# Key and query products of the state joined to two Gram products, and the second joins to the other two, in a fused DeltaNet and maxout kernel

## The chip, the cores and the metric

The kernel runs on one core of one Trainium2 chip. The metric is the device time of one execution in microseconds. Before the change, three runs took 506.8 us in the median (504.97 to 507.69). The profile is of one further look at an execution on that core, whose span from the first to the last instruction is 505.2 us.

The engines are called by short names: PE is TensorE (PEld its weight loads), DVE is VectorE, ACT is ScalarE, POOL is GpSimd, SP is SyncE, which issues most of the DMAs. PSUM is the memory that PE writes its products to, SBUF the one that all engines work in.

## The reference

Two blocks, one behind the other. First a DeltaNet recurrence over 768 positions, for 4 batches of 8 heads with 48 dimensions each:

```python
k_n = k / (norm(k) + 1e-06)
for t in range(S):
    y[t]  = q[t] @ state
    v_old = k_n[t] @ state
    state = state + beta[t] * outer(k_n[t], v[t] - v_old)
```

Then `y`, with its heads side by side, is a matrix `x` of 3072 tokens by 384, and a maxout layer follows:

```python
h = maximum(maximum(x @ w1, x @ w2), x @ w3)   # 384 -> 768
out = h @ w_out                                # 768 -> 384
```

All is float32.

## The kernel before

**Chunks.** The sequence is cut into 12 chunks of 64 positions (`C = 64`). A chunk `c` holds two units, `n = 2c + g`: a unit is one chunk of half of the batches, so there are 24 units. Within a chunk the recurrence is turned into matrix products: a Gram matrix of the keys with themselves and with the queries, a triangular system, and products with the state that the chunk before left.

**Periods.** The maxout layer works on 512 tokens at a time, which is two chunks of all batches. So there are six periods, `m = 0` to `5` (`GROUPS = 6`). `ffn(m)` is a generator for the layer of period `m`; at each `yield` the main loop (L1505 to L1525) emits what a table tells it for that step. While the layer of period `m` runs, the recurrence of period `m + 1` (its chunks `2m + 2` and `2m + 3`) is done, and the units of period `m + 2` are prepared. So every engine's order of work is written out by hand: the order in which the program emits the instructions is the order on each engine's queue.

**The layer's steps.** In the periods 1 to 4, steps 0 to 11 are one hidden product each (`hidden`, L1217): three matmuls of 128x128 weights with 512 columns into `p_h` (the profile has two records for each float32 matmul, so six). Even steps are followed by a relu on ACT (L1234), odd ones by a maximum on DVE (L1238), which free the PSUM buffer; `p_h` has two buffers. Behind them come the products with `w_out` into `p_o`. In period 1, steps 2 and 5 have twelve records of `p_m` (L905) in addition, put between the hidden product and the table's names.

**The names of the tables.** Each is a letter and a number. Those that the change moves, and those around them:

- `k0` (`old_k`, L750): the keys of the period's first chunk times the state, 64 records of 48x64 tiles into `p_k`, and a subtraction on DVE (L755) that makes the right side. Nothing is done for it on a DMA queue.
- `q0` (`old_q`, L759): the same with the queries, 64 records into `p_q`, and a copy on ACT (L763).
- `g0` to `g3` (`gram`, L404): the Gram products of four units to come; the even ones 32 records of 128 columns, the odd ones 64 of 64 columns, into `p_g`. Then the mask on DVE (L399), a copy to `at` on ACT (L432), and four DMAs on SP (L445) that write `at` to memory.
- `t0` to `t3` (`turn_blocks`, L384): four transposes on DVE that make the `kqt` of the unit whose Gram product follows.
- `z0 z1` (`join_z`, L706): 64 records of 32x32 tiles each into `p_z`, and two copies on ACT.
- `j0 j1` (`join_u`, L719): the second joins, 64 records of 32x32 tiles each into `p_j`, and two ACT instructions each (L728) that write the negated product into `ut`.
- `d0 d1` (`turn_t1`): transposes on DVE that `j0 j1` read.
- `u0` (`new`, L765): the solved values, 64 records into `p_u`; it reads `ut` (behind `j0`) and the right side (behind `k0`).
- `s0`, `y0`, `k1`, `q1`, `u1` and so on: the state's step, the outputs, and the same for the second chunk.
- `L3`, `N0` to `N2`: loads of units to come (`load_blocks`, a memset and DMAs on POOL, partly on SP). `V0 V1`: loads of values.

At step 6 of a period `blocks` (L487) reads the Grams of `at` back in another layout into `x_bl`, on SP; at step 8 `solve` (L507) begins on them, a long row of small DVE instructions (L561, L565) which go on through the rest of the period.

**PSUM.** All of the recurrence's products take one of three buffers in turn (`ps_two`, tag `two`, L92). A product has to wait until what was in its buffer three products before has been read.

**The table.** `LINKS` (L1380) serves the periods 1 and 2. `FOURTH_LINKS` (L1385) serves period 3 and takes its steps 0 to 13 from `LINKS`. Period 0 has `EARLY_LINKS`, period 4 has `LAST_LINKS`; in period 5 nothing is left to do for the recurrence.

## Time and profile before

| | |
|---|---|
| three runs | 506.8 us median, 504.97 to 507.69 |
| profiled execution | 505.2 us span; its time outside the span is not shown |
| PE busy | 484.0 us, 8064 matmuls and 8064 weight loads |
| DVE busy | 361.1 us |
| ACT busy | 169.4 us |
| POOL busy | 187.1 us |
| TensorE's granted clock | 0.968 in the mean |
| the three changed periods start | at 158.35, 242.56 and 315.32 us |

The page tells for each engine how long it was busy. Further views answer for a stretch of time: the timeline lists an engine's instructions merged by line (start, length, engine, line, operation, output and inputs, tile shape, count, and in brackets the idle time before it with what ended it); the DMA view tells of each queue's packets, with their number, their megabytes and the time that they took as a share of 16 DMA engines over the stretch. Matmuls overlap in PE's pipeline, so the length of a group contains the tail of its last one, and the distance from a group's start to the next one's start is the better measure. The word "issue" stands for idle time in which an engine waited for nothing that the profile shows.

### The profile page before, as it was taken

Reading aid. Unit: us, or ns where it says so; the run is one execution under the profiler, and the core shown is the slowest. Engines: PE = TensorE matmul, PEld = TensorE weight load, DVE = VectorE, ACT = ScalarE, POOL = GpSimd, SP = SyncE. Lnnn points to the kernel's source line nnn. Section 1 sums busy time; section 2 is a strip of 40 time slices with the busy share of each in tenths; the row PEclk is TensorE's granted clock in tenths of the full one; section 3 lists DMA queues with packets and bytes.
Section 4 is the critical chain, followed back from the end, with each engine's and each line's share of the span. In section 5 each row is a group of like instructions: output and inputs, shape, how many; then the busy total and the mean of one; then the engine's idle time right before and its main releaser. Section 6 shows DMA issues by size and latency. Waiting matters only on the chain.

```text
span 505.2 us, 18676 instructions
## 1 busy us (share of the span) xinstructions
PE 484.0 (96%) x8064; PEld 338.0 (67%) x8064; DVE 361.1 (71%) x835; ACT 169.4 (34%) x320; POOL 187.1 (37%) x311
## 2 busy tenths in 40 slices
PE   7678989999999999999999999999999999999996
PEld 6467767855566555565565565555797457998895
DVE  5888799787996441799652999565998874468753
ACT  5585664885422142210152200242201032212210
POOL 7434472793391935770395880501000020000000
PEclk9855899999999999999999999999999999999999
DMA  8937869864045934544584652744224230340002
GB/s 114 205 50 214 195 142 160 198 181 137 3 120 134 191 72 77 146 119 117 112 156 104 158 137 74 149 72 96 64 54 90 47 86 15 85 94 1 0 18 47
DMA packets 109121, 53.50 MB, mean 106 GB/s; under 512 B 92208, under 2 KB 102864, under 8 KB 109040
## 3 DMA queue, kind: packets, MB, share of 16 engines
q1 hardware_dynamic: 97280, 31.78, 31.0%
q0 software_dynamic: 9216, 19.85, 16.5%
q8 instruction: 63, 1.03, 0.9%
q10 hardware_dynamic: 2544, 0.69, 0.8%
q14 instruction: 18, 0.15, 0.1%
HBM read 39.17 MB, written 13.11 MB: 103 GB/s over the span
## 4 chain that ended last, share of the span: by engine, by line
PE 76%; DVE 11%; ACT 4%; DMA 3%; SPq 3%; issue 2%; POOL 0%; DVEq 0%; ACTq 0%; POOLq 0%
PE p_h L1224 28%; PE p_o L985 13%; PE p_o L1262 12%; PE p_c L1163 5%; DVE tmp L561 3%; PE p_g L415 2%; PE p_m L905 2%; PE p_u L771 2%; PE p_k L743 2%; DVE y_p L565 2%; DMA kmore<-in_k_dram 2%; PE p_y L813 2%; PE p_s L794 2%; PE p_q L743 1%; PE p_j L726 1%
## 5 line engine op out<-in xcount | busy, mean ns | idle before, releaser
L1224 PE MATMUL p_h<-xt,w_sb 128*128 128x512 f32 (+1 forms) x450 | 186.8, 558 | 0.6 <-ACT xt L839 0.6
L1224 PEld LDWEIGHTS p_h<-xt,w_sb 128*128 128x128 f32 x450 | 82.4, 193 | 69.2 <-issue 61.6
L1238 DVE TENSOR_TENSOR h<-h,p_h 128x512 f32<-128x512 f32 (+1 forms) x42 | 25.5, 607 | 46.8 <-PE p_h L1224 46.3
L565 DVE TENSOR_TENSOR y_bl<-y_bl,tmp 128x31 f32<-128x31 f32 (+20 forms) x139 | 50.4, 363 | 4.8
L561 DVE TENSOR_TENSOR tmp<-x_bl,y_bl 128x31 f32<-128x31 f32 (+20 forms) x139 | 48.8, 351 | 3.9
L1262 PE MATMUL p_o<-wo_sb,h 128*128 128x384 f32 x144 | 48.9, 490 | 0.0
L373 POOL DMA_DIRECT2D turned<-in_q_dram x72 | 39.3, 554 | 4.6 <-POOL turned L368 3.1
L1262 PEld LDWEIGHTS p_o<-wo_sb,h 128*128 128x128 f32 x144 | 26.7, 190 | 17.2
L1234 ACT ACTIVATE h<-p_h 128x512 f32<-128x512 f32 x24 | 14.3, 597 | 69.2 <-PE p_h L1224 69.2
L263 POOL TENSOR_TENSOR w_sb<-mant,up 128x384 int32<-128x384 int32 x18 | 19.0, 1054 | 39.5 <-DVE mant L259 37.8
L415 PEld LDWEIGHTS p_g<-kqt 48*64 48x64 f32 x1216 | 24.5, 142 | 9.2 <-issue 6.3
L415 PE MATMUL p_g<-kqt 48*64 48x64 f32 (+1 forms) x1216 | 27.7, 241 | 0.9 <-ACT kqt L344 0.8
L1268 ACT COPY o_sb<-p_o 128x384 f32<-128x384 f32 x12 | 5.8, 479 | 62.6 <-PE p_o L1262 56.5
L801 DVE TENSOR_TENSOR st<-st,p_s 48x768 f32<-48x768 f32 (+1 forms) x18 | 17.1, 949 | 12.7 <-PE p_s L794 12.4
L399 DVE TENSOR_TENSOR pt<-p_g,mask 128x512 f32<-128x512 f32 x20 | 13.8, 690 | 17.0 <-PE p_g L415 16.9
L598 POOL DMA_DIRECT2D ut<-y_d x4 | 2.6, 653 | 60.6 <-DMA y_d<-y_bl 60.6
L148 POOL DMA_DIRECT2D v_t<-in_v_dram x14 | 11.6, 832 | 35.3 <-PE p_u L771 35.3
L368 POOL MEMSET turned<- 128x96 f32 x18 | 3.3, 191 | 49.4 <-DVE kqt L389 49.4
L771 PEld LDWEIGHTS p_u<-v_t,ut 64*64 64x64 f32 x768 | 13.5, 141 | 8.4 <-issue 7.3
L432 ACT COPY at<-p_g 128x512 f32<-128x512 f32 x22 | 12.8, 585 | 17.4 <-DVE pt L399 15.4
L373 POOL DMA_DIRECT2D turned<-in_k_dram x32 | 17.5, 556 | 1.2 <-POOL turned L368 1.2
L1163 PE MATMUL p_c<-xt,w_sb 128*128 128x256 f32 x72 | 17.7, 379 | 0.0
(239 smaller groups left out, 907.3 us busy)
## 6 DMA issues: line engine op xcount, KB each, us to landing
w_bits<-in_moe_w_dram SPq DMA_DIRECT2D x9, 384.0 KB, 6.2
w_bits<-in_moe_w_dram POOLq DMA_DIRECT2D x9, 384.0 KB, 5.7
turned<-in_q_dram POOLq DMA_DIRECT2D x72, 48.0 KB, 2.8
out_dram<-o_sb SPq DMA_DIRECT2D x36, 96.0 KB, 2.3
y_x<-y SPq DMA_DIRECT2D x32, 96.0 KB, 3.0
qall<-y_x SPq DMA_DIRECT2D x32, 96.0 KB, 2.8
v_t<-in_v_dram POOLq DMA_DIRECT2D x14, 192.0 KB, 5.0
at_d<-at SPq DMA_DIRECT2D x72, 32.0 KB, 3.0
```

The source lines that it names most:

```text
L263: nc.gpsimd.tensor_tensor(out=dst.bitcast(I32), in0=mant_v.bitcast(I32), in1=up_v, op=ALU.add)
L373: (queue, nc.gpsimd)[i].dma_start(out=t[p0 : p0 + 32, bb, at : at + NP * 2 * D].rearrange("p (j x) -> p j x", j=NP), in_=(k, q)[i][2 * bb ...
L415: nc.tensor.matmul(p_g[rows(bb ^ (g * i)), par, c0 : c0 + C * (1 + whole)], kq[:, 0], kq if whole else kq[:, i],)
L561: nc.vector.tensor_tensor(out=t_v, in0=row.to_broadcast(t_v.shape), in1=column.to_broadcast(t_v.shape), op=ALU.mult,)
L565: nc.vector.tensor_tensor(out=rest, in0=rest, in1=t_v, op=ALU.subtract)
L771: nc.tensor.matmul(p_v[rows(bb ^ g), g, i], ut[c % NU][rows(bb), g, h], rhs[rows(bb), g, h],)
L801: nc.vector.tensor_tensor(out=s_v[r], in0=s_v[r], in1=p_s[r, :, 0 : H * D], op=ALU.add)
L985: nc.tensor.matmul(to[:, g], a[j][:, 128 * g : 128 * (g + 1)], b[j], start=(start and g == j == 0), stop=(stop and g == 1 and j == len(a) ...
L1163: nc.tensor.matmul(to, w[stays], moves, start=(n == 0), stop=(n == len(terms) - 1))
L1224: nc.tensor.matmul(p_h, w_sb[i][:, t, f * 128 : (f + 1) * 128], xt[:, t, lo : lo + w], start=(t == 0), stop=(t == KT - 1),)
L1238: nc.vector.tensor_tensor(out=h, in0=h, in1=p_h, op=ALU.max)
L1262: nc.tensor.matmul(p_o, stays, moves, start=(n == 0), stop=(n == len(terms) - 1))
```

## The change

Four names move in `LINKS`. `k0 q0` leave step 0 and stand in front of `g0 g1` in step 2; `j0 j1` leave step 4 and stand in front of `g2 g3` in step 5. Their order among themselves and towards the other products stays. Between two hidden products the recurrence puts a run of small tiled products on PE; a period had ten such runs and now has eight. Since `FOURTH_LINKS` takes over the steps 0 to 13, the change holds for the periods 1, 2 and 3.

```diff
     LINKS = {
-        0: "k0 q0 t0 L3", 1: "t1", 2: "g0 g1 t2", 3: "z0 z1 d0 d1", 4: "j0 j1 t3 V0",
-        5: "g2 g3 p1", 6: "u0 N0", 7: "V1 N1", 8: "s0 y0 N2", 9: "x0", 10: "k1 q1",
+        0: "t0 L3", 1: "t1", 2: "k0 q0 g0 g1 t2", 3: "z0 z1 d0 d1", 4: "t3 V0",
+        5: "j0 j1 g2 g3 p1", 6: "u0 N0", 7: "V1 N1", 8: "s0 y0 N2", 9: "x0", 10: "k1 q1",
         11: "u1 w0", 13: "y1 x1 s1", 14: "X0 w1", 16: "P0", 17: "X1 K0 K1 K2 K3",
     }
```

No function changes.

## The prediction

> **What bounds the kernel now.** I read the page first, then the chain of waits, then TensorE's timeline through one period, then the packets that bring TensorE its instructions.

> ```profile
> span 505.2 us, 18676 instructions
> PE 484.0 (96%) x8064; PEld 338.0 (67%) x8064; DVE 361.1 (71%) x835; ACT 169.4 (34%) x320; POOL 187.1 (37%) x311
> ...
> q8 instruction: 63, 1.03, 0.9%
> ...
> PE 76%; DVE 11%; ACT 4%; DMA 3%; SPq 3%; issue 2%; POOL 0%; DVEq 0%; ACTq 0%; POOLq 0%
> ```

> PE is busy for 96% of the span, and from 131 us on the chain that ended last lies on PE almost alone, so whatever PE gains or loses in the three changed periods reaches the end. The third line is the one that I weigh most. 63 packets of 16 KB (1.03 MB / 63) stand against 8064 weight loads and 8064 matmuls: 16128 / 63 = 256 instructions a packet. TensorE is fed in blocks of 256.

> The second of the three changed periods, on PE:

> ```profile
> 245.23 1.15 PE L743 MATMUL p_k<-st,kqt 48*64 48x48 f32 x64
> 246.20 1.11 PE L743 MATMUL p_q<-st,kqt 48*64 48x48 f32 x64
> 247.24 5.42 PE L1224 MATMUL p_h<-xt,w_sb 128*128 128x512 f32 x12
> 252.59 2.09 PE L415 MATMUL p_g<-kqt 48*64 48x128 f32 x96
> 254.61 2.84 PE L1224 MATMUL p_h<-xt,w_sb 128*128 128x512 f32 x6
> 257.38 1.35 PE L713 MATMUL p_z<-ut,at 32*32 32x32 f32 x128
> 258.66 2.84 PE L1224 MATMUL p_h<-xt,w_sb 128*128 128x512 f32 x6
> 261.43 1.63 PE L726 MATMUL p_j<-z,t 32*32 32x32 f32 x128
> 263.00 2.84 PE L1224 MATMUL p_h<-xt,w_sb 128*128 128x512 f32 x6
> 265.77 2.09 PE L415 MATMUL p_g<-kqt 48*64 48x128 f32 x96
> ```

> Each row starts where the one before ends: PE waits for no engine here. Two things are to be seen. A run of p_h between tiled runs takes 2.77 us for six records, while twelve in one piece take 5.35, not 5.54. And the tiled rows hold many short instructions: p_j has 128 matmuls and as many loads, 256 instructions or one whole block, in 1.4 to 1.6 us, where p_h needs 2.77 us for twelve. The p_j row is also uneven: 1.39, 1.56 and 1.42 us from its start to the next row in the three periods, against 1.28 for p_z of the same shape.

> One stall shows what can lie behind that:

> ```profile
> 63.73 0.91 PE L771 MATMUL p_u<-v_t,ut 64*64 64x48 f32 x47
> 65.65 0.49 PE L771 MATMUL p_u<-v_t,ut 64*64 64x48 f32 x17 [1.01 <-issue]
> ```

> PE stops for 1 us in the middle of p_u and waits for nothing that the profile names. Counted in order of time (loads, matmuls and PE's own waits), the instruction behind the gap is number 2753 = 11 x 256 - 63. The largest gap inside the p_j of 261.43 (0.19 us, at 261.87) is at 9409 = 37 x 256 - 63, and the one inside the p_j of 334.19 (at 334.95) at 11969 = 47 x 256 - 63. Three gaps at one place of the block are no accident: PE came to a block that was not there yet. The packets before them, in narrow windows of the DMA view (62.8 to 64.5 us, then 259.1 to 260.5):

> ```profile
> q8 instruction: 1, 0.02, 5.5%
> ...
> q8 instruction: 1, 0.02, 4.9%
> ```

> 5.5% of 16 engines over 1.7 us is a packet of 1.5 us, 4.9% over 1.4 us one of 1.1. They landed at 64.38 and 260.32; PE went on at 65.65 and 261.87, 1.27 and 1.55 us later.

> **The change part by part.** It adds and removes no instruction; k0 q0 and j0 j1 go behind later steps of p_h in three periods (m = 1, 2 and 3; the others have tables of their own).

> What leaves PE. Starts of p_h are 0.429 us apart, 0.523 before a tiled run and 0.533 after one (+0.094, +0.104). The last p_q is followed by p_h after 0.148 us, but p_k by p_q after 0.038 (+0.110); the first four p_g take 0.140, later ones 0.089 (+0.051). Joining k, q and g saves all four, 0.36 us. Joining j and g saves the first two, 0.20 us: where a p_j of 32x32 tiles is followed directly by a 48x64 product (61.16 us) its exit costs 0.121 and the entry 0.035 more, as towards p_h. So 0.56 a period, 1.67 us in three; 2.15 at most if p_j to p_g were free as well.

> What comes. Runs of 448 instructions (k q g g: 128+128+192; j j g g: 256+192) in 3.9 and 3.4 us, where none before was over 256 without a p_h behind it in these periods. Price of a block, from the three gaps: block entered to next packet's start 1.51 (261.87 to 263.38), 1.29 and 1.19, mean 1.33; a packet 1.27 (mean of the six around the gaps, 1.11 to 1.50); landing to use 1.41 (the two above). Together 4.0 us. The packets often start before PE reaches the block, in slow p_h by some 40 instructions, which inside a tiled run is worth 0.25 us. So a block that PE runs through in less than 3.75 us makes it wait for the rest. Before, neighbouring blocks of the stretch are entered 3.99 to 4.95 us apart at the tightest (177.19 to 181.18, 257.69 to 261.87 to 266.27, 330.82 to 334.95): just enough.

> I moved the records into the new order and marked every 256th. First period: blocks begin at the end of q and near the end of j (120th of 128), and p_h steps stand inside both: 5.0 and 5.3 us, no wait. Second: one begins at the 23rd matmul of j, the next at the 21st of g: 1.14 + 0.15 + 0.58 = 1.87 us, a wait of 1.9. Third: 50th of k to 50th of g, 0.21 + 0.93 + 0.99 + 0.26 = 2.4, a wait of 1.35; 61st of j to 60th of g, 2.35, a wait of 1.4. Sum 4.65 us. A fourth pair (11th of k to 11th of g in the second period, 2.0 us) is asked for while p_h still runs, so I take 0 for it; without that lead it costs 1.7. With the quickest terms seen (0.8 + 0.93 + 1.27 = 3.0 us) the three come to 1.6; with the slowest (4.3 us) and the fourth, to 7.7. The waits fall in g; p_h, the relu and max behind it and the z or u products wait with PE, nothing overtakes.

> [...]

> Costed at nothing, with their cover:

> ```profile
> 246.50 0.95 DVE L755 TENSOR_TENSOR v_t<-v_t,p_k 128x768 f32<-128x768 f32 x1 [2.33 <-PE p_k L743]
> 262.42 2.40 ACT L728 ACTIVATE ut<-p_j 32x512 f32<-32x512 f32 x4 [0.29 <-PE p_j L726]
> 280.47 0.26 ACT L270 ACTIVATE root_bl<-x_bl 128x32 f32<-128x32 f32 x1 [1.85 <-DMA x_bl<-at_d]
> 285.12 0.68 DVE L1238 TENSOR_TENSOR h<-h,p_h 128x512 f32<-128x512 f32 x1
> ```

> The pool of three PSUM buffers is taken in the same order as before, but closer. g1 takes p_k's: free 1.27 + 0.95 = 2.2 us after k starts, wanted after 0.97 + 0.93 + 0.99 = 2.9. g3 takes p_j0's: free after two of ACT's four 0.6 us copies, 2.2, wanted after 2.5. If ACT were one copy late, 0.3 us a period. g2's copy to `at` starts behind those four, 3.4 us after j starts, and its mask on DVE ends then too, so the DMA of the Grams and x_bl move by 0 to 0.2 us; x_bl's root is needed at 280.86, and the max that frees p_h ends at 285.80 for a matmul at 286.16, so 0.36 us covers that. The moved products issue no DMA, so the order on SP's and POOL's queues stays. t0's transposes lose k0's 0.95 us in front of them; POOL's memset behind them and its loads start earlier, beside the loads of ut, which end by 256.0 (last issue 251.75, slowest landing 4.2) for a z at 257.38: 1.4 us of cover. u needs j0 and k0 only after another p_h.

> Sum: -1.67 + 4.65 = +3.0 on the profiled span of 505.2, so 508.2. The three runs have a median of 506.8 (504.97 to 507.69), 1.6 above that span, so 509.8.

> **The rivals.** (1) The blocks come in time, because more than one is held ahead: 506.8 - 1.7 = 505.1, not slower. It decides if a block takes under 1.9 us from entry to use of the next. For it: 384 instructions in one piece at 124.7 to 127.7 us (p_k, p_y, p_q) show no gap. Against it: only one block's edge falls in that piece, and the three gaps. If the uneven p_j (0.11 + 0.28 + 0.14 us over p_z) became even and p_j to p_g were free, 2.15 + 0.53 = 2.7, so 504.1. [...] (2) A PSUM buffer or x_bl is late in place of blocks: three times 0.3 to 0.6 us against 1.7, so 506.0 to 506.9. Nothing in the rows is late yet. (3) All block edges find slow packets, four waits: -1.7 + 7.7 = +6.0, so 512.8; it is the far end of my own case.

> **How the numbers follow.** Blocks late: 0.72, from 506.7 (-1.67 + 1.6) to 512.8, likeliest 509.8. Rival 1: 0.22. Rival 2: 0.06. 0.5% is 2.5 us, about what a measurement of this kernel can tell from no change. Late blocks give 0.66 slower and 0.06 within; rival 1 0.12 within and 0.10 faster; rival 2 0.06 within. The range 505.0 to 512.8 leaves out half of rival 1 and a little at the top; the likeliest case alone is 507 to 512.8.

> **What would show it.** Right: p_h runs of eighteen and twelve records in one piece, p_k and p_q before p_g without a gap; then gaps of 1 to 2 us marked issue inside p_g of the second and third period, an instruction packet ending 1.3 to 1.6 us before each ends. Wrong: p_g still 2.0 us after p_q and p_j (rival 1), or p_g released by ACT or DVE (rival 2).

## The result

The changed kernel takes 514.83 us in the median of six runs (511.67 to 518.16), the kernel before 507.22 us (504.97 to 508.74, six runs): a ratio of 1.0159, 95% interval 1.0121 to 1.0197. It is slower by 1.6% or 7.6 us, where +3.0 us (509.8 us) were predicted, and it lies above the range's end of 512.8 us. The profiled execution took 511.67 us, the least of the six; its span is 510.0 us.

From the page of the changed kernel, the lines that answer to the first fence of before:

```profile
span 510.0 us, 18668 instructions
PE 484.1 (95%) x8064; PEld 338.5 (66%) x8064; DVE 364.0 (71%) x835; ACT 168.9 (33%) x320; POOL 187.1 (37%) x311
...
q8 instruction: 63, 1.03, 0.9%
...
PE 81%; DVE 6%; DMA 5%; issue 2%; SPq 2%; ACT 2%; POOL 0%; DVEq 0%; ACTq 0%; POOLq 0%
```

PE is busy for as long as before (484.1 us against 484.0); the span is longer. So PE works no slower in this execution, it waits more. The timeline of PE in the second period shows where (start, length, engine, line, operation, tiles; in brackets the idle time before and what ended it):

```profile
252.08 1.15 PE L743 MATMUL p_k<-st,kqt 48*64 48x48 f32 x64
253.05 1.11 PE L743 MATMUL p_q<-st,kqt 48*64 48x48 f32 x64
253.98 2.06 PE L415 MATMUL p_g<-kqt 48*64 48x128 f32 x96
255.97 2.84 PE L1224 MATMUL p_h<-xt,w_sb 128*128 128x512 f32 x6
258.74 1.35 PE L713 MATMUL p_z<-ut,at 32*32 32x32 f32 x128
260.02 5.42 PE L1224 MATMUL p_h<-xt,w_sb 128*128 128x512 f32 x12
265.37 1.52 PE L726 MATMUL p_j<-z,t 32*32 32x32 f32 x128
266.82 0.88 PE L415 MATMUL p_g<-kqt 48*64 48x128 f32 x23
268.95 1.44 PE L415 MATMUL p_g<-kqt 48*64 48x128 f32 x73 [1.26 <-issue]
270.32 1.55 PE L1224 MATMUL p_h<-xt,w_sb 128*128 128x512 f32 x3
```

The two joined runs are there, and the second one, j with g, breaks in two after 23 records of p_g. The matmul behind the break is PE instruction 9665 of the program in order of time, and 9665 = 38 x 256 - 63: a block's edge. One instruction packet lies in front of it, the first row here, from the DMA view of 266.3 to 267.8 us:

```profile
q8 instruction: 1, 0.02, 5.2%
```

It was on its way from 266.42 to 267.66; PE went on at 268.95, 1.29 us after the landing. The view of PE's waits between 240 and 350 us has one line, where that of before has none:

```profile
PE p_g L415 <- issue: 3.5, 3, 1.4
```

3.5 us in all, three times, 1.4 at the longest: the one above and two in the third period, inside the 96 records of p_g behind k q (at 329.85) and behind j (at 344.50). No engine, no PSUM buffer and no `x_bl` is named.

For what follows I use one measure, the **stretch** from the first hidden product of period 1 to the first of period 4. It holds the three changed periods and nothing else. In before's profile it is 227.32 us, here 229.76: +2.44. The other 2.35 us by which the span grew lie ahead of it, in code that the change does not touch (period 1 starts at 160.70 us, before at 158.35). Behind it both need 119.5 us.

### The profile page after: what moved, and what is told of

It is laid out like the page before. It is cut to its first block, busy times and chain, and to the rows that moved or that the text cites. A ratio compares the mean times of both kernels' runs of the same rounds, so it can differ in the third digit from the quotient of the medians.

```text
span 510.0 us, 18668 instructions
## 1 busy us (share of the span) xinstructions
PE 484.1 (95%) x8064; PEld 338.5 (66%) x8064; DVE 364.0 (71%) x835; ACT 168.9 (33%) x320; POOL 187.1 (37%) x311
## 3 DMA queue, kind: packets, MB, share of 16 engines
q8 instruction: 63, 1.03, 0.9%
## 4 chain that ended last, share of the span: by engine, by line
PE 81%; DVE 6%; DMA 5%; issue 2%; SPq 2%; ACT 2%; POOL 0%; DVEq 0%; ACTq 0%; POOLq 0%
PE p_h L1224 31%; PE p_o L985 12%; PE p_o L1262 12%; PE p_c L1163 5%; PE p_u L771 3%; PE p_g L415 3%; PE p_y L813 3%; PE p_m L905 2%; PE p_k L743 2%; PE p_q L743 2%; DMA kmore<-in_k_dram 2%; PE p_j L726 2%; PE p_s L794 1%; DMA qall<-in_q_dram 1%; DVE tmp L561 1%
## 5 line engine op out<-in xcount | busy, mean ns | idle before, releaser
L1224 PE MATMUL p_h<-xt,w_sb 128*128 128x512 f32 (+1 forms) x450 | 186.2, 558 | 1.8 <-issue 1.2
L1224 PEld LDWEIGHTS p_h<-xt,w_sb 128*128 128x128 f32 x450 | 82.8, 193 | 73.9 <-issue 67.0
L1238 DVE TENSOR_TENSOR h<-h,p_h 128x512 f32<-128x512 f32 (+1 forms) x42 | 25.5, 607 | 47.4 <-PE p_h L1224 43.8
L415 PE MATMUL p_g<-kqt 48*64 48x64 f32 (+1 forms) x1216 | 29.0, 245 | 4.4 <-issue 3.5
L415 PEld LDWEIGHTS p_g<-kqt 48*64 48x64 f32 x1216 | 25.4, 145 | 9.4 <-issue 6.6
L771 PEld LDWEIGHTS p_u<-v_t,ut 64*64 64x64 f32 x768 | 13.5, 141 | 9.2 <-issue 8.1
L247 ACT ACTIVATE mant<-w_bits 128x384 f32<-128x384 f32 x24 | 13.5, 562 | 12.7 <-POOL w_sb L263 6.1
```

Source lines behind the costliest of these rows:

```text
L415: nc.tensor.matmul(p_g[rows(bb ^ (g * i)), par, c0 : c0 + C * (1 + whole)], kq[:, 0], kq if whole else kq[:, i],)
L771: nc.tensor.matmul(p_v[rows(bb ^ g), g, i], ut[c % NU][rows(bb), g, h], rhs[rows(bb), g, h],)
L1224: nc.tensor.matmul(p_h, w_sb[i][:, t, f * 128 : (f + 1) * 128], xt[:, t, lo : lo + w], start=(t == 0), stop=(t == KT - 1),)
L1238: nc.vector.tensor_tensor(out=h, in0=h, in1=p_h, op=ALU.max)
```

## The experiments

My theory stood as in the prediction: PE reaches a block of 256 instructions before it has been brought. Its rivals now: the joined order costs time by itself, wherever the edges lie; or the excess over the profile's +2.4 us has another cause altogether, since the runs say +7.6.

### The same two programs again

No edit. The changed kernel:

> The changed kernel once more, to see what of its loss is the same in every execution. From the first p_h of period 1 to the first p_h of period 4 it took 229.76 us in the first profile, 227.32 before the change. Blocks late: again 229 to 231 us, with gaps of 1 to 1.7 us inside p_g at the 23rd record of the second joined run of period 2, the 52nd of the first and the 62nd of the second joined run of period 3, and none in period 1. What is over in the median of the runs (7.6 us against 4.8 between the two profiles) would then be lost in front of period 1 or behind period 4, or in a lower clock. If the gaps are chance (a rival), they stand elsewhere or are missing.

> The changed kernel a third time, for the spread of its waits: the medians of the two sets of runs (514.83 and 513.55 us) ask for a stretch from period 1 to period 4 of about 227.3 + 5 = 232 us, and the first profile showed 229.8, the second 232.7. Block theory: gaps at the block edges inside p_g at the same three records (23rd of the second period, 52nd and 62nd of the third) and nowhere else in the three periods, each 1.1 to 2.7 us, and half clock in just those windows of 3.41 us that follow a window with under about 2 us of work, none of it a hidden product; the stretch is 227.3 - 1.7 + the gaps + 1.3 us for each spell. Rival, the rest of the excess has another cause: a stretch over 231 us with gaps that sum to under 5 us and no half clock, or gaps away from block edges.

> The changed kernel a fourth time, with the same expectations as the third. Of four executions, block theory with the window of 3.41 us expects one or two with a spell of half clock in the second or third period.

and the kernel before:

> The kernel before once more, for how much two executions of one program differ. Block theory: no gap of over 0.5 us at a block's edge in the three periods, the stretch from the first hidden product of period 1 to that of period 4 within 0.3 us of 227.3 us, and no spell of half clock in it; what differs lies in the first 160 us (there the five traces so far range from 158.35 to 162.92 us with the same instructions). Rival, noise everywhere: the stretch itself moves by 2 to 5 us, as it did between the two traces of the changed kernel (229.8 and 232.7).

> The kernel before a third time. Block theory: a stretch from period 1 to period 4 of 227.1 to 227.4 us, as in the two others, no gap of over 0.5 us in it, no half clock; the start of period 1 anywhere from 158 to 163 us. Rival: a stretch that differs by over 1 us.

The first repeat was timed in six runs: 513.55 us (511.30 to 516.58) against 507.45, ratio 1.0118 (1.0083 to 1.0154). The others are single executions, of 517.33 and 514.79 us (changed) and of 511.05 and 506.96 us (before). The stretches:

| | stretch, us |
|---|---|
| before, three executions | 227.32, 227.10, 227.32 |
| changed, four executions | 229.76, 232.69, 234.06, 235.18 |

Before repeats to 0.2 us; the changed kernel does not. Its four executions wait at the same three records; the fourth waits in p_z of period 2 as well. What else they show, as distances from the start of a row to the start of the next one:

| row | usual | profile | second | third | fourth |
|---|---|---|---|---|---|
| p_g behind j, period 2 | 1.99 | 3.51 | 4.23 | 5.09 | 4.45 |
| p_g behind k q, period 3 | 1.99 | 3.14 | 4.24 | 4.24 | 4.32 |
| p_g behind j, period 3 | 1.99 | 3.69 | 3.39 | 3.42 | 3.29 |
| six p_h behind the first row | 2.77 | 2.77 | 3.94 | 4.52 | 3.58 |
| six p_h behind the second row | 2.77 | 2.77 | 2.77 | 2.77 | 4.47 |
| p_z, period 2 | 1.28 | 1.28 | 1.52 | 1.44 | 2.54 |
| sum over the usual | | 4.37 | 7.30 | 8.69 | 9.86 |

The sums less 1.9 us (what the joins save, below) are 2.5, 5.4, 6.8 and 8.0; the stretches are 2.5, 5.4, 6.8 and 7.9 us over before's mean of 227.25. So these six rows hold the whole loss, 5.7 us in the mean, and the profile had shown the mildest case of four. The gaps at the three edges alone, from the start of one record to the start of the next, sum to 4.23, 5.30, 5.56 and 5.17 us.

The rows of p_h are the news. From the fourth execution's timeline, period 3:

```profile
328.19 1.40 PE L415 MATMUL p_g<-kqt 48*64 48x128 f32 x52
331.65 0.93 PE L415 MATMUL p_g<-kqt 48*64 48x64 f32 x44 [2.06 <-issue]
332.51 4.54 PE L1224 MATMUL p_h<-xt,w_sb 128*128 128x512 f32 x6
```

and its table of stretches of time (length, then busy time and instructions of PE, PEld, DVE, ACT and POOL, the granted clock, the DMA share, GB/s):

```profile
329.80:333.22 3.42, 1.57 (x46) 1.27 (x47) 0.80 (x2) 0.58 (x1) 0.00 (x0) 1.00 0.92 146
333.22:336.63 3.41, 3.41 (x5) 1.03 (x4) 1.44 (x5) 0.58 (x1) 0.00 (x0) 0.50 0.29 53
```

After the wait of 2 us the clock is granted at 0.50 for 3.41 us, and p_h takes 0.85 us a record, not 0.43. A wait is paid once as a wait and, in four of the twelve cases, a second time as half clock. All timed runs point the same way: the granted clock is 0.961 in the mean of the twelve timed runs of the changed kernel, and 0.967 in the twenty of the kernel before that were timed with the second six. By these two means that is some 6 us more at half clock in an execution, an estimate (0.006 of 510 us, at half a clock lost); the four traces have 0, 3.4, 6.8 and 6.8 us of it in the stretch, those of before none.

The expectation of the second execution was missed: 232.69 us in place of 229 to 231, and gaps of 1.81, 2.19 and 1.30 us in place of 1 to 1.7. That of the third and fourth held for the three records and the sizes of their gaps. It did not hold for the late p_z of the fourth, nor for the windows ahead of half clock, one of which had 2.48 us of work and one 0.71 us of hidden products (the table further down). Spells came in three of four executions, where I had asked for one or two.

### One half of the change at a time

Only k and q move:

```diff
-        0: "k0 q0 t0 L3", 1: "t1", 2: "g0 g1 t2", 3: "z0 z1 d0 d1", 4: "j0 j1 t3 V0",
+        0: "t0 L3", 1: "t1", 2: "k0 q0 g0 g1 t2", 3: "z0 z1 d0 d1", 4: "j0 j1 t3 V0",
```

> Only k0 q0 are moved in front of g0 g1; the joins stay alone. Blocks late: 1.03 us saved in three periods, and one gap of about 1.1 us inside p_g of period 3 (the other two runs of k q g have one block's edge, or an edge asked for early): 227.3 to 227.6 us from the first p_h of period 1 to that of period 4, three gaps less two. Rival, that a PSUM buffer or the work behind a joined run is late: a loss in each of the three periods, with p_g or the next p_h released by ACT or DVE.

Only the second joins move:

```diff
-        0: "k0 q0 t0 L3", 1: "t1", 2: "g0 g1 t2", 3: "z0 z1 d0 d1", 4: "j0 j1 t3 V0",
-        5: "g2 g3 p1", 6: "u0 N0", 7: "V1 N1", 8: "s0 y0 N2", 9: "x0", 10: "k1 q1",
+        0: "k0 q0 t0 L3", 1: "t1", 2: "g0 g1 t2", 3: "z0 z1 d0 d1", 4: "t3 V0",
+        5: "j0 j1 g2 g3 p1", 6: "u0 N0", 7: "V1 N1", 8: "s0 y0 N2", 9: "x0", 10: "k1 q1",
```

> Only j0 j1 are moved in front of g2 g3. Blocks late: 0.6 us saved and two gaps of 1.4 to 1.7 us inside p_g, in periods 2 and 3 and not in period 1: 229.5 to 230 us for the stretch. Rival (PSUM buffer or the work behind late): a loss in each of the three periods.

With j alone the stretch is 230.13 us (514.21 us, 507.41 to 515.49 in nine runs; ratio 1.0082, 1.0040 to 1.0124), with waits at the two places of the j runs; a maximum that was 0.8 us late adds the second line. The nine runs fall into two groups, three of up to 508.93 us and six from 513.46 us on, so their median says little; the traced one is of the second group, and its period 1 starts late already (162.92 us). With k q alone it is 232.02 us (509.85 us, 507.27 to 513.74 in twelve runs; ratio 1.0053, 1.0027 to 1.0079). PE's waits between 155 and 360 us, first of j alone, then of k q alone:

```profile
PE p_g L415 <- issue: 2.3, 2, 1.2
PE p_h L1224 <- DVE h L1238: 0.8, 1, 0.8
```

```profile
PE p_g L415 <- issue: 2.5, 1, 2.5
PE p_z L713 <- issue: 0.7, 1, 0.7
PE p_z L713 <- DMA ut<-y_d: 0.5, 1, 0.5
```

Each half saves its part in period 1 (0.31 and 0.34 us) and loses more later. The second one missed its expectation by over 4 us: one wait of 2.5 us in place of about 1.1, half clock behind it (the first p_h records 1.01, 0.85, 0.85 and 0.69 us apart, 1.6 us more than usual), and two waits of p_z. Neither half is worth taking in all three periods.

### The block edges moved

Small products that nothing reads, put on PE early in the program, shift every later edge: 50 of them, each two loads and two matmuls (200 PE instructions), or 8 of them (32).

```diff
+    p_w = ps_ffn([128, TOK], "p_w")
+    for n in range(50):
+        r = slice(32 * (n % 4), 32 * (n % 4 + 1))
+        nc.tensor.matmul(p_w[r, 0:BL], ident[r, r], ident[r, r])
```

With 50 in the changed kernel, so that two edges fall into each of the six joined runs:

> The changed kernel with 50 small matmuls (200 instructions) more on TensorE ahead of everything, so that every block of 256 begins 200 instructions earlier in the work; order, waits and data of the three periods are as they were. Blocks late: six gaps in place of three, one in each joined run of all three periods, 1.2 to 2 us each, 233 to 235 us for the stretch. If the place of the blocks does not matter (rival: late PSUM buffers, or the order itself): 229.8 us and gaps at the same records as before.

With 50 in the kernel before:

> The kernel before with the 50 small products (200 PE instructions) of the run that moved all edges of the changed kernel, but in the order before the change. Block theory: without joined runs the edges may lie anywhere, neighbouring edges stay 4 us apart, so a stretch of 227.3 to 227.9 us. Rival, the added products (or the moved edges as such) cost the time: 229 us or more, against 233.7 with both.

With 8 in the changed kernel (`range(8)` in the same lines):

> The changed kernel with 8 small products (32 PE instructions, a result that nothing reads) added after the first busy stretch of identity products, so that every later block's edge falls 32 instructions earlier in the program's order; the table is that of the change. Block theory: in the second period the edges leave the joined run of j and g (one falls into the hidden product ahead of it), so there is no wait there and the way from the first hidden product of period 1 to that of period 3 is 1.1 us shorter than before's 156.97, 155.9 us (after: 157.15 and 159.28); in the third period two waits stay, 1.2 and 1.5 us, so the stretch to period 4 is 228.3 us, or 229.6 if one of them brings a spell of half clock; time 1.0 to 2.3 us above the kernel before. Rival, the joined order itself costs the time, wherever the edges are: gaps in the second period as in the changed kernel and a stretch of 229.8 to 232.7 us, 5 to 7 us above the kernel before.

The stretches are 233.74 us (changed, 50; the median of four runs is 519.97 us, ratio 1.0258, 1.0217 to 1.0299), 228.40 us (before, 50) and 233.23 us (changed, 8; 512.67 us, 510.53 to 515.12 in seven runs, ratio 1.0091, 1.0059 to 1.0124). The 50 products also come ahead of period 1, which starts at 163.66 and 164.28 us with them, so the stretch tells more here than the times. PE's waits from 155 to 360 us in the three, in this order:

```profile
PE p_g L415 <- issue: 5.0, 5, 2.1
```

```profile
PE p_z L713 <- issue: 0.7, 1, 0.7
```

```profile
PE p_g L415 <- issue: 2.6, 3, 1.4
PE p_h L1224 <- issue: 1.5, 1, 1.5
PE p_z L713 <- issue: 0.7, 1, 0.7
```

The waits go where the edges go. With 50 products period 1, which never waited, has one small wait (0.16 us idle, in its first joined run), and the second and third have two each, at other records than in the changed kernel. In all kernels every gap marked "issue" in these periods lies before instruction 256 n - 63 or the one behind it. These places rule out the rival that the order alone costs the time, and so does period 1, which gains 0.65 us by the joined order where it holds no wait. The sums of the stretches alone could not do it: 2.5 to 7.9 us are lost with the kernel's own edges, 6.5 and 6.0 with these.

The sizes were a different matter. Of the six gaps of 1.2 to 2 us that I expected with 50 products five came, of 0.43, 1.23, 1.15, 2.36 and 0.93 us from start to start. The sixth pair of edges, in the second joined run of period 1, lies 1.64 us apart (193.26 and 194.90) and costs nothing: its packet had started 0.54 us before PE entered the block, behind slow p_m records. With 8 the stretch of 233.23 us is far above the expected 228.3 to 229.6. The pair in the second period came apart as expected, but 1.4 us of small waits stayed there, and a wait of 1.67 us over the usual distance appeared in period 1 where I expected none:

```profile
176.54 1.35 PE L713 MATMUL p_z<-ut,at 32*32 32x32 f32 x128
177.82 1.13 PE L1224 MATMUL p_h<-xt,w_sb 128*128 128x512 f32 x2
180.46 1.55 PE L1224 MATMUL p_h<-xt,w_sb 128*128 128x512 f32 x3 [1.50 <-issue]
```

Here one block begins at the start of p_z, whose 128 loads and 128 matmuls fill it almost exactly. It lasts 2.2 us, the next block's packet starts 1.55 us after it was entered, and PE stops between two records of p_h. No run was joined at this place, and the kernel before, shifted by 50, also gets a wait (0.9 us in p_z of period 3; 228.40 us against the expected 227.3 to 227.9). So a joined run is not the only shape that outruns the blocks; before's edges lie well.

### A wait without an edge

To see what half clock follows, PE was made to wait for ACT in the kernel before, ahead of the third Gram product of each period:

```diff
+    def held_gram(n):
+        if n % 4 == 2:
+            whole = kqts[n].rearrange("p j b i t -> p (j b i t)")
+            for _ in range(3):
+                nc.scalar.copy(whole, whole)
+        gram(n, queues=(nc.gpsimd,) * 2 if n in (10, 11) else one_queue)
-    UNIT.update(t=turn_blocks, K=lambda n: load_k(n, one_queue if n > 19 else (nc.gpsimd, nc.gpsimd)))
+    UNIT.update(t=turn_blocks, g=held_gram, K=lambda n: load_k(n, one_queue if n > 19 else (nc.gpsimd, nc.gpsimd)))
```

> The kernel before, with three copies of a transposed block onto itself on ACT (1.03 us each) ahead of the third Gram product in each of the three periods, which lets PE wait there about 2.2 us for ACT, at no block's edge. It separates a wait of PE from a late block. If any PE wait of this length halves the granted clock: three spells of half clock of 3.3 us, each behind a wait, each 1.2 to 1.7 us, a stretch of 227.3 + 3 x 2.2 + 3 x 1.4 = 238 us. If the half clock comes only with late instruction blocks: no spell, 233.9 us, hidden products 0.43 us apart right behind the wait.

It takes 523.86 us (521.78 to 526.63, four runs; ratio 1.0318, 1.0269 to 1.0366), the stretch 238.79 us. That is the first theory's 238, but made of other parts: the waits are 3.67, 2.23 and 2.23 us, and only the first has half clock behind it, for two windows. Around the second wait, from the table of stretches of time:

```profile
275.33:278.75 3.42, 1.62 (x4) 0.38 (x2) 0.69 (x1) 3.33 (x4) 1.59 (x3) 1.00 0.36 75
278.75:282.16 3.41, 2.98 (x98) 2.44 (x99) 1.38 (x2) 1.07 (x3) 0.00 (x0) 1.00 0.02 5
```

PE worked 1.62 us in the first window and kept its clock. The changed kernel, shifted by 8, worked longer and lost it:

```profile
326.47:329.89 3.42, 2.00 (x105) 1.87 (x101) 1.23 (x2) 1.38 (x2) 0.94 (x1) 1.00 1.05 171
329.89:333.30 3.41, 3.41 (x36) 1.85 (x28) 2.02 (x5) 0.58 (x1) 0.00 (x0) 0.50 0.40 84
```

So it is neither every wait of some length nor late blocks as such. Within each trace, all changes of the granted clock lie a multiple of 3.413 us apart (in before's profile they are at 5.31, 18.96, 22.38, 25.79, 53.10 and 503.65 us, in the changed kernel's at 4.89, 15.13, 42.44, 66.33, 69.74, 107.29 and 110.70); the windows above were cut at that phase. What PE did in a window, and the clock of the next:

| kernel, window from | PE busy, us | of it in 128x128 tiles | next clock |
|---|---|---|---|
| held, 193.41 | 0.09 | 0.09 | 0.50 |
| k q alone, 327.67 | 0.95 | 0 | 0.50 |
| changed, V0 later (below), 267.22 | 1.10 | 0 | 0.50 |
| changed, shifted by 50, 333.17 | 1.27 | 0 | 0.50 |
| changed, fourth, 329.80 | 1.57 | 0.71 | 0.50 |
| changed, second, 266.70 | 1.87 | 0 | 0.50 |
| changed, fourth, 264.95 | 1.99 | 0 | 0.50 |
| changed, shifted by 8, 326.47 | 2.00 | 0 | 0.50 |
| changed, third, 266.74 | 2.48 | 0.27 | 0.50 |
| held, 350.43 | 1.50 | 1.50 | 1.00 |
| held, 275.33 | 1.62 | 1.62 | 1.00 |
| changed, second, 331.55 | 2.01 | 1.16 | 1.00 |
| changed, profile, 342.81 | 2.03 | 1.03 | 1.00 |
| changed, third, 331.59 | 2.23 | 0 | 1.00 |

Small tiles seem to count for less than 128x128 ones: windows with nothing else and up to 2.0 us of work lost the clock all six times, while 1.5 and 1.6 us of hidden products kept it. The second window of half clock in the held kernel fits this, with 3.08 us of small products and half clock once more behind it:

```profile
196.83:200.24 3.41, 3.08 (x82) 3.08 (x86) 0.69 (x1) 0.58 (x2) 0.00 (x0) 0.50 0.00 0
```

The bound is not sharp (2.48 us lost the clock, 2.23 kept it), and that the size of the tiles decides was not tested by itself. Whether a wait of 2 us was paid twice thus went with what stood around it and with how it lay to a grid whose phase differed between the executions (in before's profile 1.90 us behind a multiple of 3.413, in the changed kernel's 1.48, in its second execution 0.46, in its fourth 2.12). That is a part of why four executions of one program differ by 5.4 us: between the sums of the first and the fourth, 2.5 us are slow p_h, 1.7 the p_g rows and 1.3 p_z. Half clock followed gaps of 1.6 to 2.7 us, and in the held kernel a wait of 3.67.

### The load on the DMA engines

The first wait of period 3 was 2.2 us in three of four executions, not 1.35. The packets in question start 1.66 to 1.94 us after PE has entered the block before, with a DMA share of 0.94 to 1.09. In the next kernel two loads of 192 KB on POOL's queue, which lie at that place, are emitted three steps later; PE's order stays that of the change:

```diff
-        0: "t0 L3", 1: "t1", 2: "k0 q0 g0 g1 t2", 3: "z0 z1 d0 d1", 4: "t3 V0",
-        5: "j0 j1 g2 g3 p1", 6: "u0 N0", 7: "V1 N1", 8: "s0 y0 N2", 9: "x0", 10: "k1 q1",
+        0: "t0 L3", 1: "t1", 2: "k0 q0 g0 g1 t2", 3: "z0 z1 d0 d1", 4: "t3",
+        5: "j0 j1 g2 g3 p1", 6: "u0 N0", 7: "V0 V1 N1", 8: "s0 y0 N2", 9: "x0", 10: "k1 q1",
```

> The changed kernel with V0, two loads of 192 KB of values on POOL's queue, moved from step 4 to step 7 of the three periods. POOL runs ahead of PE, so in the changed kernel these loads lie at 326 to 330 us, around the packet that PE waits for inside the first p_g run of period 3; now they come behind the loads of N0. PE's order is the same. If the DMA load makes that packet late: its start comes 1.0 to 1.3 us after the block is asked for, not 1.7 to 1.9, the gap at the 52nd p_g is 1.1 to 1.6 us, not 2.2, no half clock behind it, and the stretch is about 1 us shorter than in the changed kernel's mean (232.9). If it does not: the gap stays at 2.2 us and the stretch at 231 to 235.

> The same once more, for the spread, with the same expectations.

The stretches are 230.37 and 232.47 us; the median of seven runs is 512.76 us (509.46 to 515.83), ratio 1.0093 (1.0062 to 1.0124). Per edge: start of the packet after the block's entry, DMA share in between, and the gap, all in us but the share:

| edge | changed, four executions | with V0 later, two |
|---|---|---|
| p_g behind j, period 2: start | 0.86, 1.05, 1.54, 1.07 | 1.53, 1.59 |
| share | 0.67, 0.73, 0.47, 0.60 | 1.20, 0.90 |
| gap | 1.53, 1.81, 2.05, 1.69 | 2.17, 2.60 |
| p_g behind k q, period 3: start | 0.58, 1.66, 1.88, 1.94 | 1.37, 1.51 |
| share | 0.83, 1.08, 0.94, 1.09 | 0.71, 1.02 |
| gap | 1.10, 2.19, 2.19, 2.28 | 1.44, 1.59 |
| p_g behind j, period 3: start | 1.20, 1.08, 1.11, 0.99 | 0.66, 0.66 |
| share | 0.00, 0.00, 0.06, 0.07 | 0.00, 0.00 |
| gap | 1.60, 1.30, 1.32, 1.20 | 0.95, 0.95 |

From the timeline of the second of the two:

```profile
266.33 0.88 PE L415 MATMUL p_g<-kqt 48*64 48x128 f32 x23
269.54 1.63 PE L415 MATMUL p_g<-kqt 48*64 48x128 f32 x73 [2.33 <-issue]
271.10 4.29 PE L1224 MATMUL p_h<-xt,w_sb 128*128 128x512 f32 x6
```

Where the two loads went can be read on POOL. In period 3, in the changed kernel (fourth execution) and then in the first with V0 later:

```profile
325.78 1.64 POOL L148 DMA_DIRECT2D v_t<-in_v_dram  x2
```

```profile
324.23 1.67 POOL L148 DMA_DIRECT2D v_t<-in_v_dram  x2
```

The blocks ahead of the wait are entered at 327.04 and 324.06 us. So the loads did not leave this place: the first of them is issued 0.2 us behind the entry, no longer 1.0 to 1.3 us ahead of it. The share stayed at 0.71 and 1.02, the packet starts fell to 1.4 and 1.5 us only, not to the expected 1.0 to 1.3, and the wait to the expected 1.1 to 1.6 us; but the profile of the changed kernel has 1.10 us with the loads ahead. In period 2 the same loads were issued over 12 us ahead of the entry at the j edge, and are now 2.4 to 2.8 us ahead of it. There the wait rose above all four of the changed kernel, with half clock behind it once (p_h 4.29 us).

Two executions thus show longer waits at the edge to which a load was brought. That the load alone makes a packet late is not shown: the last edge has starts of 0.66 and of 1.0 to 1.2 us with empty engines. The stretch is 1.5 us shorter in the mean, less than the executions differ among themselves.

### Joins only where no pair of edges falls

First, k q joined in the periods 1 and 2 and j in period 1, period 3 as before:

```diff
-        0: "k0 q0 t0 L3", 1: "t1", 2: "g0 g1 t2", 3: "z0 z1 d0 d1", 4: "j0 j1 t3 V0",
+        0: "t0 L3", 1: "t1", 2: "k0 q0 g0 g1 t2", 3: "z0 z1 d0 d1", 4: "j0 j1 t3 V0",
...
+    JOINED_LINKS = {**LINKS, 4: "t3 V0", 5: "j0 j1 g2 g3 p1"}
     FOURTH_LINKS = {
-        **LINKS, 14: "w1", 15: "X0", 16: "", 17: "", 18: "X1",
+        **LINKS, 0: "k0 q0 t0 L3", 2: "g0 g1 t2", 14: "w1", 15: "X0", 16: "", 17: "", 18: "X1",
...
-            late = {GROUPS - 3: FOURTH_LINKS, GROUPS - 2: LAST_LINKS}
+            late = {1: JOINED_LINKS, GROUPS - 3: FOURTH_LINKS, GROUPS - 2: LAST_LINKS}
```

> Only the joined runs that hold no pair of block edges: k q in front of g in the periods 1 and 2, j in front of g in period 1 alone, period 3 as before the change. Block theory: no wait at a block's edge, three joins saved (0.36 + 0.36 + 0.20 us), a stretch of 226.4 us against 227.3, and a time 0.9 us below the kernel before. Rival, joined runs cost by themselves: period 1 saves its 0.6 us as seen, but period 2 shows gaps in the joined run of k q and g, and the stretch is 228 us or more, 1 us or more above the kernel before.

508.05 us (504.62 to 511.35, twelve runs) against 508.65, ratio 0.9985 (0.9951 to 1.0019); the stretch is 227.15 us. No joined run waits, but most of the gain (0.8 of the expected 0.9 us) is lost behind them, at the next two edges of the second period (PE's waits, 155 to 360 us):

```profile
PE p_j L726 <- issue: 0.3, 1, 0.3
PE p_z L713 <- issue: 0.3, 1, 0.3
```

Their packets start 2.35 and 2.01 us after the blocks are entered. Then the change in period 1 alone:

```diff
+    JOINED_LINKS = {
+        **LINKS, 0: "t0 L3", 2: "k0 q0 g0 g1 t2", 4: "t3 V0", 5: "j0 j1 g2 g3 p1",
+    }
-            late = {GROUPS - 3: FOURTH_LINKS, GROUPS - 2: LAST_LINKS}
+            late = {1: JOINED_LINKS, GROUPS - 3: FOURTH_LINKS, GROUPS - 2: LAST_LINKS}
```

> The change in period 1 alone, where no joined run holds a pair of block edges; the periods 2 and 3 as before. Block theory: 15.58 and 16.57 us for the steps 0 to 3 and 3 to 6 of period 1 (before: 15.92 and 16.88), all later stages as before, no gap at a block's edge, a stretch of 226.6 us against 227.1 to 227.3. Rival, the joins are paid back later in the same or the next period: a stretch of 227.1 us or more.

The stretch is 226.60 us, as expected to the last digit: steps 0 to 3 in 15.58 us, 3 to 6 in 16.57, all else as before, no wait of PE from 155 to 360 us. The join itself is worth 0.65 us a period. One execution took 506.83 us; a gain of 0.13% is below what a comparison of run times tells here, so this version is shorter in its stretch and not proven faster in its time.

## Why the prediction was wrong in size

**What bounds the kernel: right.** PE's busy time did not change in the profile, and every microsecond that PE waited in the stretch came out in the span; the 119.5 us behind it were the same in all these kernels to 0.2 us.

**What leaves PE: nearly right.** 1.67 us were predicted for three periods. Period 1 shows 0.34 us for k q (predicted 0.36) and 0.31 us for j (predicted 0.20): 0.65, or 1.9 us in three. The 0.11 us more is the uneven p_j of period 1, 1.28 us in place of 1.39 once its edge fell elsewhere, which I had put into the first rival alone.

**Where the waits fall: right.** Three waits were predicted, at the 21st p_g of the second run of period 2, the 50th and the 60th of period 3; they are at the 23rd, the 52nd and the 62nd. None in period 1, and none at the fourth pair in any of four executions, since its packet had started in the slow p_h ahead of it, as taken (in the profile at 250.95 us, the block before was entered at 252.25).

**Their size: right in the profile, low in the mean.** 4.65 us were predicted; the gaps sum to 4.23 us in the profile and 5.07 in the mean of four. The terms "1.33 to the packet's start, 1.27 for the packet, 1.41 from landing to use" came out as 0.58 to 1.94, 0.88 to 1.41 and 1.23 to 1.57 at the twelve edges. The start is the term that spreads, and I had taken the mean of three at other edges for a place where the DMA engines carry 0.83 to 1.09 of their full share. The trace of before had shown more: the packet that ended the stall at 65.65 us started 1.94 us after its block was entered (60.94 to 62.88). Two readings beside it were wrong as well. Blocks in the stretch are entered 3.99 us apart "at the tightest" only among tiled runs; two follow each other in 3.31 us (294.29 and 297.60) without a wait, since the packet had started 2.7 us before the entry, in slow p_o. And the far end of 7.7 us does not come out of its terms: 4.3 us a block give 8.6 us, and 7.6 with the lead of 0.25 us taken off.

**The step that failed is the overlap behind a wait, and with it the sum, which had no term for half clock.** "p_h, the relu and max behind it and the z or u products wait with PE, nothing overtakes" assumed that work behind a wait goes on at its old pace. In three of four executions it did not. Of the mean excess of 7.56 us in the rows, 5.07 are gaps, 1.36 are p_h at half clock, 0.7 are the rest of the p_g rows (0.15 in the profile, which has no half clock there), and 0.42 are p_z. The trace of before has half clock only ahead of 53 us and behind PE's last product, and I took that for a part of the start; what makes it come back was never asked. The top of the range, 512.8, was built from a fourth wait that never came and had no room for this term.

**Costed at nothing.** The PSUM buffers, the masks, `x_bl` and the relu and maximum held in the changed kernel: PE's waits name none of them. The cover of 1.4 us for `ut` before p_z did not always hold: in the fourth execution PE waits 0.7 us there for the loads of `ut`, and 0.2 us for a block.

```profile
PE p_g L415 <- issue: 4.5, 3, 2.1
PE p_z L713 <- DMA ut<-y_d: 0.7, 1, 0.7
PE p_z L713 <- issue: 0.2, 1, 0.2
```

The p_z row costs 0.42 us in the mean of four; 0 was taken.

**The rivals.** Blocks that come in time (505.1 us) are refuted by the waits that move with the edges; that more than one block is held ahead, no run showed. A late buffer did not occur. The third, all edges with slow packets (512.8 us), is nearest in its time and wrong in its make-up.

**What stays open.** The sum of the mean case, as the traces give it, is -1.9 + 5.1 + 2.1 + 0.4 = +5.7 us, or 512.5 us on the 506.8 us that the prediction started from: still inside its range, by 0.3 us. The run medians differ by 7.6 and 6.1 us in the two sets. The remainder of 0.4 to 1.9 us is of the size that four executions leave open, whose stretches scatter by 2.3 us (1.2 us for their mean, an estimate). It is also of the size by which the start of period 1 varies in one and the same program (158.35, 162.73 and 158.38 us in before; 160.70, 160.57, 162.07 and 158.37 in the changed kernel). That the change causes it was not shown, and no instruction ahead of period 1 differs.

## What to carry to other kernels

Count instructions as well as microseconds when short products are put side by side: PE here got them in packets of 256, and mostly 3.2 to 4.7 us passed from entering one block to the use of the next (up to 6 with a DMA share of 0.9 to 1.2); where it passed 256 quicker than that it waited, joined or not, unless slow products just ahead had let the packet start early (0.54 us before the block was entered behind p_m, 2.7 us in p_o). Put long products between two edges, mark where every 256th instruction falls before an order is changed, and expect the same order to cost differently when instructions are added ahead of it (6.0 us over before's stretch with 32 more here, 6.5 with 200, 2.5 to 7.9 with none). Price a wait twice where small tiles surround it: once as a wait, and once more for the clock (0.8 to 1.8 us, in four of twelve cases here); and read such a change from several executions, since one profile showed 2.4 us of a loss of 5.7.
